# A decode attention block on one core: V as the stationary operand in every step, q broadcast and outputs written step by step

## The chip, the cores and the metric

The kernel runs on 1 core of one Trainium2 chip. The metric is the device time in microseconds of one execution; before the change the median of 3 runs is 1302.78 us (1302.27 to 1303.64).

A core has five engines with one instruction stream each: TensorE (PE; its weight loads are shown as PEld), VectorE (DVE), ScalarE (ACT), GpSimd (POOL) and SyncE (SP), which here issues nearly all transfers. They are ordered against each other by semaphores only. Transfers between HBM and the core's SBUF are carried out by sixteen DMA engines.

## The reference, cut to what matters

Eight sequences decode one token each. Attention has 32 heads, 4096 cached keys and a head size of 128; beside it stands a small MLP; all is bf16.

```python
def _A_ref(x, k_cache, v_cache, wq, wo):          # x (8,1,640), caches (8,32,4096,128)
    q = (x @ wq).reshape(B, Sq, Hq, Dh).transpose(0, 2, 1, 3)
    scores = jnp.einsum("bhqd,bhkd->bhqk", q, k) * (Dh ** -0.5)
    p = _softmax(scores, axis=-1)
    o = jnp.einsum("bhqk,bhkd->bhqd", p, v)
    return o.transpose(0, 2, 1, 3).reshape(B, Sq, Hq * Dh) @ wo

def _B_ref(x, w1, b1, w2, b2):
    y = _layernorm(x, axis=-1)
    h = _gelu(jnp.einsum("bsd,df->bsf", y, w1) + b1)
    return jnp.einsum("bsf,fd->bsd", h, w2) + b2

xn = _layernorm(x, axis=-1)
return x + _A_ref(xn, A_k_cache, A_v_cache, A_wq, A_wo) + _B_ref(xn, B_w1, B_b1, B_w2, B_b2)
```

The two caches are 2 x 268 MB; each element of them is used once.

## The kernel before

The work on the caches is cut into 64 steps (`NQ`): one step is one sequence `b` and a group of four heads (`HS`), 8 groups (`hq`) times 8 sequences. A step has 4 MiB of K and 4 MiB of V. Partition p holds head p // 32 and 128 consecutive keys of it, `j` = 0 to 127, so that `K_sb[p, slot, j, :]` is one key. K and V have two slots each (`i % 2`).

The keys of a step are shared by two ways to the scores. VectorE takes the first 88 (`dve_chunk`, four chunks of 22): it multiplies K by a q that is broadcast to the partitions of its head (`qbc_sb`), adds the two halves, and reduces. TensorE takes the last 40, in five tiles of 8 keys: `pe_T` transposes them to PSUM, `act_T` copies them to SBUF (`KT_sb`, `NS` = 4 buffers), `pe_QK` multiplies them by the four q columns, and `act_S` brings the scores home. `dve_max` finds the maximum per head over both shares, `act_exp` writes exp into `P_sb` and, by the accumulator, its row sums; `pe_RS` adds these over the partitions and `dve_rinv` inverts.

The product with V has P as the stationary operand: in `pe_PV` one matmul takes four keys of all partitions (`NA` = 32 matmuls of 512 columns in a step, issued in 8 groups), with a stationary operand of 16 columns, head by key. Of the 16 x 512 result only the blocks where the two key numbers agree are wanted: `act_E` evicts and scales it, and `pe_ex` picks the blocks with four small matmuls, into `OT_ps`. When the eight sequences of a head group are done, `cp_o` copies `OT_ps` out; `pe_ot` and `cp_ot` transpose it into rows of `O_sb`, and after seven groups `pe_ox` and `cp_ox` turn these into `oX_sb`, the stationary operand for the first 28 heads of `wo`. The last step (63) is written apart (`last_RS`, `last_PV`, `last_on` and others): there V is stationary, with 128 weight loads and a moving operand of 4 columns each, and the result is normalised on VectorE.

The q broadcast is made once for a head group: `qrep` on GpSimd repeats q along 32 columns for all 8 sequences (1024 columns), and two calls of `qbc` transpose it with matmuls, four sequences each, and copy it to `qbc_sb`.

The order on all engines is written by hand. `at(pos, fn)` gives each piece a position, step i lying at 100 i, and the pieces are recorded in the order of their positions. A recorder (`_Eng`) keeps each engine's list of calls and adds the waits, and `_replay` writes each list out. So an engine that waits at one piece holds up all that is later on its own list. On SP, K of step i is at 100 i - 90 and waits until step i - 2 is done with that slot (its transposes and VectorE's products), V of step i is at 100 i + 20 and waits for PV of step i - 2. The first part of `wo` (`load_woa`, 14 heads) is at 6222, behind V of step 62, and waits for `pe_ox`; V of step 63 is at 6320 in three pieces, and then come `wob` and the other four parts of `wo`. TensorE's list has in each step the transposes and QK tiles (from 100 i + 5), the q broadcast where one is due (+42), the row sums of the step before (+56), and its PV (+60). At the end stand `fin_b` and `fin_woa(0)`, the row sums and PV of step 63, `fin_wob` and the other `fin_woa`, and the store.

Of the kernel before, what the change touches and what calls it, by code (L numbers as in the profile page):

```python
# [92 lines left out]

def _replay(e, calls):
    for name, a, k, inc in calls:
        if name == "wait_ge":
            e.wait_ge(*a, **k)
            continue
        inst = getattr(e, name)(*a, **k)  # L99
        if inc is not None:  # L100
            inst.then_inc(*inc)


def bass_parallel_sum__gqa_block_cached__mixer_channel_mlp__decode_kernel(
# [28 lines left out]
    NPVG = 8  # L133
    NHA = H - HS
    NA = NKEY // 4
    assert NKEY == 128
    NS = 4
# [22 lines left out]
    with ExitStack() as es:  # L160
# [20 lines left out]
        P_sb = sb("P_sb", [P, 2, NA, HS, 4], BF)  # L181
        E_sb = sb("E_sb", [HS * 4, 2, 4 * DH], BF)
        qT_sb = sb("qT_sb", [P, H, B], BF)
        qrep_sb = sb("qrep_sb", [P, B, HS, HP], BF)
        qbc_sb = sb("qbc_sb", [P, 2, B, DH], BF)
        oTn_sb = sb("oTn_sb", [P, 2, HS, B], BF)
# [13 lines left out]
        mask_sb = sb("mask_sb", [P, HS * 4], F32)  # L200
# [6 lines left out]
        rs_sb = sb("rs_sb", [P, 2], F32)  # L207
        rs4_sb = sb("rs4_sb", [P, HS], F32)
        ri4_sb = sb("ri4_sb", [P, HS], F32)
        ones_f = sb("ones_f", [P, P], F32)  # L210
        rinv_sb = sb("rinv_sb", [HS * 4, 2], F32)
# [11 lines left out]
        OT_ps = CH_ps[:, 0:B * HS]  # L223
        RS_ps = CH_ps[0:HS * 4, 32:33]
# [71 lines left out]
        def consts_pool():  # L296
            tk["iota"] = pool.sig(pool.iota(iota_i[:, :], [[1, P]], base=0, channel_multiplier=-1))
            pool.memset(mask_sb[:, :], 0.0)
            pool.memset(zeros_sb[:, :], 0.0)
            pool.memset(ones_sb[:, :], 1.0)  # L300
            pool.memset(mx_sb[:, :], 0.0)
            pool.memset(rs4_sb[:, :], 0.0)
            pool.memset(ones_f[:, :], 1.0)
            t = pool.sig(pool.memset(nsc_sb[:, :], -SCALE))
            pool.wait(t)
            for h in range(HS):
                t = pool.sig(pool.memset(mask_sb[h * HP:(h + 1) * HP, h * 4:(h + 1) * 4], 1.0))
            tk["consts"] = t
            pool.wait(t)
            tk["pz"] = pool.sig(pool.memset(P_sb[:, :, :, :, :].rearrange("p n a h s -> p (n a h s)"), 0.0))  # L310
# [61 lines left out]
        def qrep(hq):  # L372
            pool.wait(tk[("q", hq * HS)], tk.get(("qb_pe", hq - 1)))
            tk[("qrep", hq)] = pool.sig(pool.tensor_copy(
                qrep_sb[:, :, :, :],
                qT_sb[:, hq * HS:(hq + 1) * HS, :].rearrange("p h b -> p b h")[:, :, :, None].to_broadcast(
                    [P, B, HS, HP])))

        def qbc(hq, half):
            k = trn[0] % 2  # L380
            trn[0] += 1
            pe.wait(tk[("qrep", hq)], tk["id"])
            TRB[k].use(pe)
            for bb in range(4):
                last = pe.matmul(TRF[:, k, bb * P:(bb + 1) * P],
                                 qrep_sb[:, half * 4 + bb, :, :].rearrange("p h r -> p (h r)"),
                                 ident_bf[:, :], start=True, stop=True)
            t = TRB[k].used(pe, pe.sig(last))
            tk[("qb_pe", hq)] = t
            act.wait(tk.get(("km", (hq - 1) * B - 1)))  # L390
            TRB[k].use(act)
            tk[("qb", hq, half)] = TRB[k].used(act, act.sig(act.activation(
                qbc_sb[:, hq % 2, half * 4:half * 4 + 4, :].rearrange("p b d -> p (b d)"),
                TRF[:, k, :], ACT.Copy)))
# [22 lines left out]
        def pe_QK(i, t):  # L417
            n = bank0[i] + t
            hq, b = divmod(i, B)
            s = i % 2  # L420
            pe.wait(tk[("ev", n)], tk[("q", hq * HS)])
            if t == 0:
                SB_[s].use(pe)
            for jj in range(TPB):
                c0 = (t * TPB + jj) * HS
                last = pe.matmul(S_ps[:, s, c0:c0 + HS], KT_sb[:, n % NS, jj, :],
                                 qT_sb[:, hq * HS:(hq + 1) * HS, b], start=True, stop=True)
            tk[("qk", n)] = SB_[s].used(pe, pe.sig(last))

# [10 lines left out]
        def dve_chunk(i, c):  # L440
            hq, b = divmod(i, B)
# [4 lines left out]
            dve.wait(piece_of("k", i, lo, hi), tk[("qb", hq, b // 4)], tk.get(("ya", n - 1)))  # L446
            tm = dve.sig(dve.tensor_tensor(
                Y_sb[:, 0:w, :], K_sb[:, s, lo:hi, :],
                qbc_sb[:, hq % 2, b, :][:, None, :].to_broadcast([P, w, DH]), ALU.mult))
# [23 lines left out]
        def act_exp(i):  # L473
            s = i % 2
            act.wait(tk[("nb", i)], tk.get(("pv", i - 2)), tk.get(("rs", i - 2)), tk["pz"])
            last_q = i == NQ - 1
            for h in range(HS):
                r = slice(h * HP, (h + 1) * HP)
                dst = (P_sb[r, s, :, :, :].rearrange("p a h s -> p (a h s)").rearrange(
                    "p (a s h) -> p a s h", s=4, h=HS)[:, :, :, h] if last_q else P_sb[r, s, :, h, :])  # L480
                last = act.activation(dst, Sd_sb[r, s, :].rearrange("p (a s) -> p a s", s=4),
                                      ACT.Exp, bias=NB_sb[r, s, 0:1], scale=SCALE,
                                      accum_out=rs4_sb[r, h:h + 1] if last_q else rs_sb[r, s:s + 1])
            tk[("exp", i)] = act.sig(last)

        def pe_RS(i):
            s = i % 2
            pe.wait(tk[("exp", i)])
            CHB.use(pe)
            tk[("rs", i)] = CHB.used(pe, pe.sig(pe.matmul(  # L490
                RS_ps, mask_sb[:, :], rs_sb[:, s:s + 1], start=True, stop=True)))

        def dve_rinv(i):
            CHB.use(dve)
            dve.wait(tk.get(("e", i - 2)))
            tk[("ri", i)] = CHB.used(dve, dve.sig(dve.reciprocal(rinv_sb[:, i % 2:i % 2 + 1], RS_ps)))


        def pe_PV(i, g):
            s = i % 2  # L500
            w = NA // NPVG
            if g == 0:
                pe.wait(tk[("exp", i)])
                PVB[s].use(pe)
            pe.wait(piece_of("v", i, g * w * 4, (g + 1) * w * 4))
            for a in range(g * w, (g + 1) * w):
                last = pe.matmul(PV_ps[0:HS * 4, s, :], P_sb[:, s, a, :, :].rearrange("p h s -> p (h s)"),
                                 V_sb[:, s, 4 * a:4 * a + 4, :].rearrange("p j d -> p (j d)"),
                                 start=(a == 0), stop=(a == NA - 1))
            if g == NPVG - 1:  # L510
                tk[("pv", i)] = PVB[s].used(pe, pe.sig(last))

        def act_E(i):
            s = i % 2
            act.wait(tk[("ri", i)], tk.get(("ex", i - 2)))
            PVB[s].use(act)
            tk[("e", i)] = PVB[s].used(act, act.sig(act.activation(
                E_sb[:, s, :], PV_ps[0:HS * 4, s, :], ACT.Copy, scale=rinv_sb[:, s:s + 1])))

        def pe_ex(i):  # L520
            s, b = i % 2, i % B
            pe.wait(tk[("e", i)], tk["id"])
            CHB.use(pe)
            for m in range(4):
                last = pe.matmul(OT_ps[:, b * HS:(b + 1) * HS], E_sb[:, s, m * P:(m + 1) * P],
                                 ident_bf[0:HS * 4, m:HS * 4:4], start=(m == 0), stop=(m == 3))
            tk[("ex", i)] = CHB.used(pe, pe.sig(last))

        def cp_o(hq):
            CHB.use(dve)  # L530
            dve.wait(tk.get(("ot", hq - 2)))
            tk[("o", hq)] = CHB.used(dve, dve.sig(dve.tensor_copy(
                oTn_sb[:, hq % 2, :, :].rearrange("p h b -> p b h"),
                OT_ps.rearrange("p (b h) -> p b h", h=HS))))

        def pe_ot(hq):
            pe.wait(tk[("o", hq)], tk["id"])
            ACCB.use(pe)
            for hh in range(HS):
                last = pe.transpose(OR_ps[0:B, hh * DH:(hh + 1) * DH], oTn_sb[:, hq % 2, hh, :], ident_bf[:, :])  # L540
            tk[("ot", hq)] = ACCB.used(pe, pe.sig(last))

        def cp_ot(hq):
            ACCB.use(act)
            act.wait(tk["mlp"])
            tk[("or", hq)] = ACCB.used(act, act.sig(act.activation(
                O_sb[:, hq * HS * DH:(hq + 1) * HS * DH], OR_ps[0:B, 0:HS * DH], ACT.Copy)))

        def pe_ox():
            pe.wait(*[tk[("or", hq)] for hq in range(NHQ - 1)])  # L550
# [9 lines left out]

        def zero_last():
            pool.wait(tk[("pv", NQ - 3)])
            tk["pz"] = pool.sig(pool.memset(
                P_sb[:, (NQ - 1) % 2, :, :, :].rearrange("p a h s -> p (a h s)"), 0.0))

        def last_RS():
            pe.wait(tk[("exp", NQ - 1)], tk["consts"])
            CHB.use(pe)
            CHB.used(pe, pe.sig(pe.matmul(CH_ps[:, 40:40 + HS], ones_f[:, :], rs4_sb[:, :],
                                          start=True, stop=True)))  # L570

        def last_rinv():
            CHB.use(dve)
            tk["ri4"] = CHB.used(dve, dve.sig(dve.reciprocal(ri4_sb[:, :], CH_ps[:, 40:40 + HS])))

        def last_PV(q):
            i, s = NQ - 1, (NQ - 1) % 2
            lo, hi = cuts("v", i)[q]
            if q == 0:
                PVB[s].use(pe)  # L580
            pe.wait(tk[("exp", i)], tk[("v", i, q)])
            ph = P_sb[:, s, :, :, :].rearrange("p a h s -> p (a h s)").rearrange("p (j h) -> p j h", h=HS)
            for j in range(lo, hi):
# [249 lines left out]
```

## Time and profile before

The profiled execution took 1300.0 us, its span (from the first to the last instruction) is 1298.2 us. Busy times are those of the span.

| | busy us | what it is mostly |
|---|---|---|
| profiled execution / its span / median of 3 runs | 1300.0 / 1298.2 / 1302.78 | |
| DVE, K times q | 410.2 in 255 instructions, 1609 ns | 22 keys each |
| DVE, reduction | 412.4 in 255, 1617 ns | |
| DVE, adding halves | 227.9 in 255, 894 ns | |
| PE, PV with P stationary | 576.6 in 2016, 512 columns | 9.4 to 9.9 us for the 32 of a step |
| PE, transposes of K | 191.5 in 2592 | |
| ACT, copies of transposed K | 317.8 in 324, 1022 ns | |
| ACT, exp | 101.6 in 256, 397 ns | |
| POOL, repeating q | 11.3 in 8, 1407 ns | |
| K load, 4 MiB | 64 loads | 24.7 us from issue to landing |
| V load, 4 MiB | 62 loads | 29.8 us from issue to landing |

A row of the costliest groups gives line, engine, operation, the tile written and those read, the shapes and the count, then the busy time and the mean duration of one in ns, and the idle time of the engine before them with what ended it. All the rows have line 99, since one helper writes every instruction; they are told apart by their tiles. Busy matmuls overlap, so the mean of one is longer than the time between two. The granted clock is the share of full speed that TensorE's clock had; its mean is 0.861.

### The profile page before, as it was taken

The numbers are of one execution on the slowest core, as the hardware profiler recorded it, in microseconds if no ns is written. First come the engines' busy times: TensorE is split into PE (matmuls) and PEld (weight loads), VectorE is DVE, ScalarE is ACT, GpSimd is POOL, SyncE is SP. The second block draws the span as 40 slices with busy tenths as digits, with TensorE's granted clock in tenths as the row PEclk, the third lists the DMA queues.
The fourth block names the chain that finished last, engine by engine and source line by source line (L and its number), as shares of the span: only waits on it lengthen the run. The fifth ranks groups of instructions, "written<-read, shape, count | busy, mean of one in ns | idle before, by whom it ended". The sixth has DMA issues, their size and how long they took to land.

```text
span 1298.2 us, 19364 instructions
## 1 busy us (share of the span) xinstructions
PE 919.8 (71%) x8239; PEld 477.8 (37%) x8239; DVE 1117.9 (86%) x1178; ACT 546.4 (42%) x1188; POOL 14.1 (1%) x26
## 2 busy tenths in 40 slices
PE   1778767767667767667767677677676677687688
PEld 1634333333333333333333333333333333343345
DVE  2998988988888988988979988888988989889883
ACT  1454353353453453453443443443543533534533
POOL 1000000000000000000000000000000000000000
PEclk9988788788888888798887888888887888888889
DMA  9999999999999999999999999999999999999997
GB/s 403 425 433 430 428 434 428 431 431 431 428 434 430 427 432 432 428 432 432 426 433 430 428 432 433 430 428 432 430 430 432 431 428 432 430 428 431 430 424 293
DMA packets 20762, 553.04 MB, mean 426 GB/s; under 512 B 2282, under 2 KB 3011, under 8 KB 3268
## 3 DMA queue, kind: packets, MB, share of 16 engines
q1 hardware_dynamic: 20642, 551.80, 99.1%
q8 instruction: 64, 1.05, 0.3%
q14 instruction: 22, 0.18, 0.0%
q10 hardware_dynamic: 34, 0.02, 0.0%
HBM read 551.80 MB, written 0.01 MB: 425 GB/s over the span
## 4 chain that ended last, share of the span: by engine, by line
DMA 67%; PE 23%; DVE 7%; ACT 2%; issue 1%; SPq 0%; DVEq 0%; ACTq 0%
DMA V_sb<-in_A_v_cache_dram 60%; PE PV_ps L99 22%; DMA K_sb<-in_A_k_cache_dram 8%; DVE Y_sb L99 4%; DVE Sd_sb L99 2%; ACT KT_sb L99 1%; PE S_ps L99 1%; ACT P_sb L99 0%; PE CH_ps L99 0%; PE TR_ps L99 0%; ACT E_sb L99 0%; DVE mx_sb L99 0%; DVE mb_sb L99 0%; DVE mxT_sb L99 0%; DVE NB_sb L99 0%
## 5 line engine op out<-in xcount | busy, mean ns | idle before, releaser
L99 PE MATMUL PV_ps<-V_sb,P_sb 128*16 128x512 bf16 x2016 | 576.6, 457 | 91.3 <-DMA V_sb<-in_A_v_cache_dram 91.3
L99 DVE TENSOR_TENSOR Y_sb<-K_sb,qbc_sb 128x2816 bf16<-128x2816 bf16 (+2 forms) x255 | 410.2, 1609 | 81.7 <-DMA K_sb<-in_A_k_cache_dram 81.6
L99 DVE TENSOR_REDUCE Sd_sb<-Y_sb 128x22 f32<-128x1408 bf16 (+2 forms) x255 | 412.4, 1617 | 8.7
L99 PEld LDWEIGHTS PV_ps<-V_sb,P_sb 128*16 128x16 bf16 x2016 | 204.3, 104 | 437.2 <-issue 183.7
L99 ACT ACTIVATE KT_sb<-TR_ps 128x1024 bf16<-128x1024 bf16 x324 | 317.8, 1022 | 78.0 <-PE TR_ps L99 76.8
L99 ACT ACTIVATE E_sb<-PV_ps,rinv_sb 16x512 bf16<-16x512 f32 x63 | 42.7, 677 | 621.6 <-PE PV_ps L99 611.4
L99 DVE TENSOR_TENSOR Y_sb<-Y_sb 128x1408 bf16<-128x1408 bf16 (+2 forms) x255 | 227.9, 894 | 8.7
L99 PE MATMUL TR_ps<-ident_bf,K_sb 128*128 128x128 bf16 x2592 | 191.5, 222 | 13.5 <-DMA K_sb<-in_A_k_cache_dram 10.7
L99 PE MATMUL S_ps<-qT_sb,KT_sb 128*128 128x4 bf16 x2592 | 118.4, 169 | 104.4 <-ACT KT_sb L99 93.7
L99 PEld LDWEIGHTS TR_ps<-ident_bf,K_sb 128*128 128x128 bf16 x2592 | 150.1, 99 | 16.0 <-DMA K_sb<-in_A_k_cache_dram 12.3
L99 PEld LDWEIGHTS S_ps<-qT_sb,KT_sb 128*128 128x128 bf16 x2592 | 89.1, 97 | 153.7 <-ACT KT_sb L99 151.7
L99 ACT ACTIVATE P_sb<-Sd_sb,NB_sb 32x128 bf16<-32x128 f32 x256 | 101.6, 397 | 7.7 <-DVE NB_sb L99 5.3
L99 PE MATMUL CH_ps<-rs_sb,mask_sb 128*16 128x1 f32 x126 | 13.0, 173 | 91.4 <-ACT P_sb L99 91.2
L99 PE MATMUL CH_ps<-ident_bf,E_sb 16*128 16x4 bf16 x252 | 15.6, 163 | 51.5 <-ACT E_sb L99 51.5
L99 ACT ACTIVATE Sd_sb<-S_ps 32x40 f32<-32x40 f32 (+2 forms) x256 | 49.7, 194 | 3.9 <-PE S_ps L99 0.5
L99 ACT ACTIVATION_READ_ACCUMULATOR P_sb<-Sd_sb,NB_sb 32x1 f32 x256 | 47.3, 185 | 0.0
L99 PEld LDWEIGHTS CH_ps<-rs_sb,mask_sb 128*16 128x16 f32 x126 | 7.5, 100 | 98.0 <-ACT P_sb L99 97.8
L99 PEld LDWEIGHTS CH_ps<-ident_bf,E_sb 16*128 16x128 bf16 x252 | 10.2, 91 | 82.4 <-ACT E_sb L99 82.4
L99 DVE TENSOR_REDUCE mx_sb<-Sd_sb 128x1 f32<-128x128 f32 x64 | 18.3, 285 | 5.9
L99 DVE CAST oTn_sb<-CH_ps 128x32 bf16<-128x32 f32 (+1 forms) x8 | 2.4, 295 | 23.4 <-PE CH_ps L99 23.4
L99 PE MATMUL CH_ps<-xT_sb,W_sb 128*128 128x8 bf16 (+1 forms) x230 | 11.1, 179 | 14.4 <-DMA W_sb<-in_A_wq_dram 10.8
L99 POOL COPY qrep_sb<-qT_sb 128x1024 bf16<-128x1024 bf16 x8 | 11.3, 1407 | 902.4 <-PE TR_ps L99 871.2
(71 smaller groups left out, 156.8 us busy)
## 6 DMA issues: line engine op xcount, KB each, us to landing
K_sb<-in_A_k_cache_dram SPq DMA_DIRECT2D x64, 4096.0 KB, 24.7
V_sb<-in_A_v_cache_dram SPq DMA_DIRECT2D x62, 4096.0 KB, 29.8
W_sb<-in_A_wq_dram SPq DMA_DIRECT2D x1, 5120.0 KB, 15.3
V_sb<-in_A_v_cache_dram SPq DMA_DIRECT2D x2, 2048.0 KB, 26.7
V_sb<-in_A_v_cache_dram SPq DMA_DIRECT2D x2, 1536.0 KB, 21.8
W_sb<-in_A_wo_dram SPq DMA_DIRECT2D x1, 2240.0 KB, 33.8
W_sb<-in_B_w_dram SPq DMA_DIRECT2D x1, 2160.0 KB, 15.7
W_sb<-in_B_w_dram SPq DMA_DIRECT2D x1, 2080.0 KB, 20.6
```

What stands on the lines that cost most here:

```text
L99: inst = getattr(e, name)(*a, **k)
```

## The change

- PV has V as the stationary operand in every step: for each of the 128 keys of a partition one weight load of V (128 x 128) and one matmul with the 4 columns of P. `P_sb` is laid out by key and then head, so exp writes every fourth element; row sums are kept per head (`rs4_sb`), and the result of `pe_RS` stands on all partitions. `act_E`, `pe_ex` and `cp_o` go; `act_O` evicts 128 x 4, and `o_norm` multiplies by the inverse sums on GpSimd (on VectorE in the last step) and writes into `oT_sb`, which has all heads.
- The q broadcast is made in every step for that step: `qrep` repeats 128 columns, `pe_qbc` transposes them with one matmul, `act_qbc` copies them. `pe_QK` takes its q columns from `qrep_sb`.
- `pe_ot` and `cp_ot` run in four groups of up to 8 heads at positions 6044 to 6185, and `pe_ox` at 6244. The first part of `wo` is at 6246. The last step no longer has functions of its own; exp of step 62 is at 6300.5, ahead of the transposes of step 63.
- `NS` is 5 instead of 4.
- A function is defined that replays a list as a loop (`_replay_loop`). It isn't called: TensorE's list is written out in full, as before. `marks` serves an assertion at build time only.

The diff, cut to its core:

```diff
@@ def qrep, qbc
-        def qrep(hq):
-            pool.wait(tk[("q", hq * HS)], tk.get(("qb_pe", hq - 1)))
...
-        def qbc(hq, half):
...
+        def qrep(i):
+            hq, b = divmod(i, B)
+            s = i % 2
+            pool.wait(tk[("q", hq * HS)], tk.get(("qb_pe", i - 2)), tk.get(("qkl", i - 2)))
+            tk[("qrep", i)] = pool.sig(pool.tensor_copy(
+                qrep_sb[:, s, :, :],
+                qT_sb[:, hq * HS:(hq + 1) * HS, b][:, :, None].to_broadcast([P, HS, HP])))
+
+        def pe_qbc(i):
             k = trn[0] % 2
             trn[0] += 1
+            pe.wait(tk[("qrep", i)], tk["id"])
             TRB[k].use(pe)
+            tk[("qb_pe", i)] = TRB[k].used(pe, pe.sig(pe.matmul(
+                TRF[:, k, 0:DH], qrep_sb[:, i % 2, :, :].rearrange("p h r -> p (h r)"),
+                ident_bf[:, :], start=True, stop=True)))
+            tk[("qbk", i)] = k
+
+        def act_qbc(i):
+            k = tk[("qbk", i)]
+            act.wait(tk.get(("km", i - 2)))
             TRB[k].use(act)
+            tk[("qb", i)] = TRB[k].used(act, act.sig(act.activation(
+                qbc_sb[:, i % 2, :], TRF[:, k, 0:DH], ACT.Copy)))
...
@@ def act_exp, pe_RS, dve_rinv, pe_PV
-                dst = (P_sb[r, s, :, :, :].rearrange("p a h s -> p (a h s)").rearrange(
-                    "p (a s h) -> p a s h", s=4, h=HS)[:, :, :, h] if last_q else P_sb[r, s, :, h, :])
-                last = act.activation(dst, Sd_sb[r, s, :].rearrange("p (a s) -> p a s", s=4),
+                last = act.activation(P_sb[r, s, :, h], Sd_sb[r, s, :],
                                       ACT.Exp, bias=NB_sb[r, s, 0:1], scale=SCALE,
-                                      accum_out=rs4_sb[r, h:h + 1] if last_q else rs_sb[r, s:s + 1])
+                                      accum_out=rs4_sb[r, s, h:h + 1])
...
-                RS_ps, mask_sb[:, :], rs_sb[:, s:s + 1], start=True, stop=True)))
+                RS_ps[:, s, :], ones_f[:, :], rs4_sb[:, s, :], start=True, stop=True)))
...
+        def pe_PV(i, q):
+            s = i % 2
+            lo, hi = cuts("v", i)[q]
+            if q == 0:
                 PVB[s].use(pe)
-            pe.wait(piece_of("v", i, g * w * 4, (g + 1) * w * 4))
-            for a in range(g * w, (g + 1) * w):
-                last = pe.matmul(PV_ps[0:HS * 4, s, :], P_sb[:, s, a, :, :].rearrange("p h s -> p (h s)"),
-                                 V_sb[:, s, 4 * a:4 * a + 4, :].rearrange("p j d -> p (j d)"),
-                                 start=(a == 0), stop=(a == NA - 1))
-            if g == NPVG - 1:
+            pe.wait(tk[("exp", i)], tk[("v", i, q)])
+            for j in range(lo, hi):
+                last = pe.matmul(PV_ps[:, s, 0:HS], V_sb[:, s, j, :], P_sb[:, s, j, :],
+                                 start=(j == 0), stop=(j == NKEY - 1))
+            if hi == NKEY:
                 tk[("pv", i)] = PVB[s].used(pe, pe.sig(last))
 
-        def act_E(i):
...
-        def pe_ex(i):
...
-        def cp_o(hq):
...
+        def act_O(i):
+            s = i % 2
+            act.wait(tk.get(("on", i - 2)))
             PVB[s].use(act)
+            tk[("oU", i)] = PVB[s].used(act, act.sig(act.activation(
+                oU_sb[:, s, :], PV_ps[:, s, 0:HS], ACT.Copy)))
+
+        def o_norm(i):
+            hq, b = divmod(i, B)
+            s = i % 2
+            dst = oT_sb[:, hq * HS:(hq + 1) * HS, b]
+            if i < NQ - 1:
+                pool.wait(tk[("oU", i)], tk[("ri", i)])
+                tk[("on", i)] = pool.sig(pool.tensor_tensor(dst, oU_sb[:, s, :], ri4_sb[:, s, :], ALU.mult))
+            else:
...
@@ the order
-                at(o + 20, load_v, i)
-            if b == 4 and hq + 1 < NHQ:
-                at(o + 50, qrep, hq + 1)
-                at(o + Q + 42, qbc, hq + 1, 0)
-                at(o + Q + 43, qbc, hq + 1, 1)
+                at(o + 20 if i != NQ - 2 else o + 20, load_v, i)
+            if i >= 1:
+                at(o - 60, qrep, i)
+                at(o - 58, pe_qbc, i)
+                at(o - 57.5, act_qbc, i)
...
-            at(o + Q + 39.5 if not last else o + 83, act_exp, i)
+            at(o + Q + 39.5 if i < NQ - 2 else o + Q + 0.5 if not last else o + 83, act_exp, i)
+            at(o + Q + 56, pe_RS, i)
+            at(o + Q + 57, dve_rinv, i)
+            for q in range(len(cuts("v", i))):
+                at(o + Q + 60 + q, pe_PV, i, q)
             if not last:
...
+                at(o + Q + 84, act_O, i)
+            at(o + Q + 88, o_norm, i)
...
-        at(o - 178, load_woa, 0)
+        for g in range(len(OTG)):
+            at(o - 356 + 47 * g, pe_ot, g)
+            at(o - 355.5 + 47 * g, cp_ot, g)
+        at(o - 156, pe_ox)
+        at(o - 155.5, cp_ox)
+        at(o - 154, load_woa, 0)
...
         @block.tensor
         def _(e):
+            assert len({y - x for x, y in zip(marks, marks[1:])}) == 1, marks
             _replay(e, pe.calls)
```

## The prediction

> **What bounds the kernel now.** First the rows of the page on transfers: the busy share in 40 slices, the rate under it, and the queues.
>
> ```profile
> span 1298.2 us, 19364 instructions
> PE 919.8 (71%) x8239; PEld 477.8 (37%) x8239; DVE 1117.9 (86%) x1178; ACT 546.4 (42%) x1188; POOL 14.1 (1%) x26
> ...
> DMA  9999999999999999999999999999999999999997
> ...
> q1 hardware_dynamic: 20642, 551.80, 99.1%
> q8 instruction: 64, 1.05, 0.3%
> ```
>
> The transfers are busy from end to end at about 430 GB/s, so no engine sets the pace; loading K and V does. The small row q8 decides this case. It carries TensorE's own program: PE and PEld have 2 x 8239 = 16,478 instructions, and 1.05 MB over 16,478 is 64 bytes each, so 64 packets of 16,384 bytes hold 256 instructions apiece (16,478 / 256 = 64.4). In the trace they come one every 20 us.
>
> Next, the table by stretches at the end (its columns: busy time and count of PE, PEld, DVE, ACT, POOL; granted clock; DMA share; GB/s).
>
> ```profile
> 1280.00:1282.00 2.00, 1.23 (x10) 0.46 (x9) 0.00 (x0) 1.28 (x5) 0.00 (x0) 1.00 0.99 402
> 1282.00:1284.00 2.00, 2.00 (x20) 1.50 (x20) 0.00 (x0) 0.00 (x0) 0.00 (x0) 1.00 0.63 263
> 1284.00:1286.00 2.00, 2.00 (x17) 1.27 (x16) 0.00 (x0) 0.00 (x0) 0.00 (x0) 1.00 0.63 259
> ...
> 1292.00:1294.00 2.00, 2.00 (x17) 1.30 (x15) 0.00 (x0) 0.00 (x0) 0.00 (x0) 1.00 0.32 118
> 1294.00:1296.00 2.00, 1.84 (x14) 0.96 (x11) 0.26 (x1) 0.13 (x1) 0.00 (x0) 1.00 0.00 0
> ```
>
> At 1282 us the share falls to 0.63, which is 10 of 16: six transfer engines are done and ten go on, the last until 1294.0. Each load leaves sixteen landing marks in the trace, one for each engine, and they tell why. At 35 us the sixteen marks of a load lie within 1.2 us of each other; at 595 us, after 29 refills, five engines are 6.1 to 6.5 us behind the first, three 4.8 to 5.0; at the end, after 64 refills, eight are 11.1 to 11.6 us behind. So the refills go round eight engines. The last mark of successive 4 MiB loads comes every 9.71 us, except around refills 9, 17, 25, 33, 41, 49 and 57, where it takes 11.10 to 11.16: a refill costs its engine 1.43 us, and the latest of the eight, hit every eighth time, sets when loads are complete.
>
> Last, the order of time on TensorE in the final 30 us:
>
> ```profile
> 1272.41 8.54 PE L99 MATMUL PV_ps<-V_sb,P_sb 128*16 128x512 bf16 x32
> ...
> 1287.15 3.37 PE L99 MATMUL PV_ps<-P_sb,V_sb 128*128 128x4 bf16 x128
> ...
> 1290.78 1.25 PE L99 MATMUL S_ps<-W_sb,oTn_sb 128*8 128x320 bf16 x8 [0.27 <-DVE oTn_sb L99]
> ...
> 1291.87 3.97 PE L99 MATMUL S_ps<-W_sb,oX_sb 128*8 128x320 bf16 x28
> ```
>
> The first row is P stationary (step 62), the second V stationary (step 63): the form that the change gives to every step is in the trace. PE ends at 1295.85, 1.9 us after the last landing.
>
> **The change, part by part.** *PV per step.* In steady state 32 matmuls take 9.4 to 9.9 us (rows at 605.07 and 624.50); 128 weight loads with 4 columns each take 3.24 us here. With a slower clock: 140 such pairs (8 columns) at 31 us, just after transposes at half pace (8 in 1.03 us, later 0.61), took 3.92 us, 28 ns a pair, so at most 3.6. TensorE gains about 6 us per step, plus 0.25 for the four extraction matmuls. What follows sooner is the next V load, which waits for PV; but the queue holds two and a half loads by then (24.7 us from K's issue to landing, at 9.71 us each), so the gain is 0. If that cover went, PE's 71% would leave the path free anyway.
>
> *TensorE's program.* 63 steps x 96 more pairs is 6048, less 252 extractions: 5796 pairs, 11,592 instructions, 45.3 more packets: 109 instead of 64. The diff defines a loop that would avoid this and does not call it. The latest engine, hit at 1, 9, ... 57 now, is hit also at 65, 73, 81, 89, 97 and 105: 6 x 1.43 = **+8.6 us** at the last landing. Bounds: five hits (7.2) or seven (10.0) if the count of waits among the instructions shifts it; and if a refill cost only its bytes, 16,384 at one engine's 4 MiB/16 per 9.71 us, it is 0.61 us, 3.6 in all. I take 1.43, since it is measured on this very queue.
>
> [...]
>
> *GpSimd.* One copy of 128 columns and one product of 4 columns per step, where there were eight copies of 1024 (1.407 us each). Bounds for each: 0.09 us (the smallest memset) to 1.41; 0.2 to 2.8 us per step on an engine that is 1% busy. I take the low end, nearer in size. They lie a step ahead: in the step shown, ScalarE copies a q broadcast at 603.02 and the next K's first product starts at 614.76, 11.7 us of cover. Behind a copy in GpSimd's queue stands only a product of a step that has long ended. Should they slow VectorE, the cover is its wait for K: 81.6 us over 54 waits, 1.5 each.
>
> *ScalarE.* Exp into every fourth element: 0.58 against 0.40 us, its accumulator read 0.25 against 0.185 (rows of steps 63 and 62): 4 x 0.245 = +1.0 per step. Evicting 128x4 instead of 16x512: 0.68 to about 0.19 (nearest row, 32x40). The q copy each step: +0.05 to +0.45. Net some +0.8 on 8.5 of 20 us; cover: PV waits 1.3 to 1.8 us for V after the row sums, and has 6 us to spare behind. *VectorE:* the reciprocal 0.146 to 0.182, seven casts go: nothing. *Head:* fewer broadcasts before K's landing at 25.8 us, which ends that wait anyway: 0.
>
> *Order at the end.* Transposes of the outputs move into steps 60 to 62, and the first wo load must wait for them, with V of step 63 and the other wo pieces behind it on SP's queue. They end about 8 us after K of step 62 lands (1242.5), so near 1250; V of step 62 keeps the late engines busy until 1271.7. 0. Exp of step 62 now precedes the transposes of step 63, so PV(62) runs early and in 3.2 us: PE then waits for landings alone. Counting from landings as now (V63 1286.9, wob 1288.5, wo pieces 1291.2, 1292.8, 1293.6, 1294.0) with 0.141 us a matmul (3.97 / 28): 8 matmuls after wob, 14 from 1291.2 to 1293.2, then 8, 4 and 2 end at 1295.2: **-0.65** against 1295.85.
>
> *Clock.* PE is then idle some 9 us before V63 lands. Against that, the profile grants 0.5 in single stretches now (0.70 as the mean of 1270 to 1275). The transposes at half pace are 1.95 times slower by their 7 intervals ((1.03 - 0.17) / (0.61 - 0.17)), so the last matmuls would take 0.275 us. Full clock: 0; all 36 at half: +3.7. I take a switch to full speed halfway, **+1.5**.
>
> [...]
>
> **Sum.** +8.6 - 0.65 + 1.5 = +9.5 us on a profiled time of 1300.0 (span 1298.2, 1.8 around it): 1309.5. The runs shown have a median of 1302.78, 2.8 above the profiled one; so 1312.3.
>
> **Rivals.** *Not slower:* V loads issued 6 us sooner let a load run faster than 9.71 us. For it: SP waits 293.6 us for PV. Against: the share stands at 0.99 to 1.03 in all stretches to 1282. 127 loads must each gain 0.075 us (0.8%) to cancel +9.5; 0.1 us would give 1299.6. Chance 0.10, two thirds of it within 0.2%. *Starved TensorE:* a V-stationary burst eats 256 instructions, a whole packet, in 3.24 us, and a packet takes 1.02 to 1.11 us once it is served; queued behind data it may come late. In mid-kernel there are 6 us for it; in the last two PV bursts each could lose 1 to 2.5: 1314 to 1317. For: no burst of that rate ran under full load yet. Chance 0.11. *VectorE as bound:* GpSimd's work at its upper price, 2.8 us per step, stretching VectorE beyond the 1.5 us that it waits: 64 x 1.3 = 83 us, 1396. Against: the operands are tiny. 0.03. *The packets spread over all sixteen engines, or count at 0.61:* +3.6 to +5, 1306 to 1308; 0.06.
>
> **How the numbers follow.** The forecast, 0.70, has its own range from five hits at full clock (7.2 - 0.65: 1309.3) to seven at half (10.0 - 0.65 + 3.7: 1315.8). Taking in the cheaper packets and the starved end gives 1306 to 1317; outside are the first rival and the third. 0.2% is 2.6 us, about what a measurement of this kernel can tell from no change: faster 0.03, same 0.08, slower 0.89.
>
> **What would show it.** q8 with about 109 packets and 1.8 MB; jumps of 1.43 us in the last marks about every eighth refill; the early engines some 19 us ahead and so idle late, a DMA share below 1 before the end; last landing near 1302.6; PV groups of 3.3 us with waits for V ahead of them. If q8 grows and the last landing stays at 1294, the price of a refill is wrong; if PV has idle time inside a burst, the second rival holds.

## The result, and the profile after

The changed kernel takes 1309.77 us (median of 5 runs, 1309.09 to 1310.56) against 1302.93 us (1302.27 to 1303.64) for the kernel before in the same comparison. The ratio is 1.0052, with a 95% interval of 1.0039 to 1.0065: about 6.8 us slower, and the interval is clear of the 0.2% that can be told from no change.

The page of the changed kernel, with the rows that answer to those shown of before (for q1, q8 and q14: packets, MB, share of sixteen engines):

```profile
span 1308.0 us, 31232 instructions
...
PE 677.6 (52%) x14035; PEld 605.4 (46%) x14035; DVE 1122.7 (86%) x1170; ACT 550.6 (42%) x1233; POOL 48.5 (4%) x139
...
PEclk9755555655555555555565555555555555555567
...
q1 hardware_dynamic: 20642, 551.80, 98.7%
q8 instruction: 110, 1.80, 0.6%
q14 instruction: 25, 0.20, 0.0%
```

TensorE has lost a quarter of its busy time, 920 to 678 us, and the kernel is slower all the same. The transfers of data (q1) are the same packets and bytes. What has grown is q8, TensorE's own program: 64 to 110 packets of 16 KB.

The end by stretches (time, busy time and count of PE, PEld, DVE, ACT, POOL; granted clock; DMA share; GB/s):

```profile
1288.00:1290.00 2.00, 2.00 (x13) 1.17 (x12) 0.00 (x0) 1.71 (x7) 0.16 (x1) 0.79 0.98 403
1290.00:1292.00 2.00, 2.00 (x17) 1.22 (x15) 0.00 (x0) 0.00 (x0) 0.06 (x1) 1.00 0.63 261
1292.00:1294.00 2.00, 1.34 (x50) 1.24 (x49) 0.18 (x1) 0.00 (x0) 0.00 (x0) 1.00 0.48 203
...
1302.00:1304.00 2.00, 2.00 (x15) 1.19 (x14) 0.00 (x0) 0.00 (x0) 0.00 (x0) 0.88 0.14 51
1304.00:1306.00 2.00, 1.62 (x12) 0.83 (x10) 0.48 (x1) 0.34 (x1) 0.00 (x0) 1.00 0.00 0
```

From 1292 us on only half of the sixteen engines (0.48) move data, for ten microseconds more; the last landing is at 1303.60. Before, it was at 1293.99. So the loss lies in front of the last landing, in the transfers, and not in TensorE's work behind it.

### The profile page after: what moved, and what is told of

It reads as the page before. It is cut to its first block, busy times and chain, and to the rows that moved or that the text cites. A ratio compares the mean times of both kernels' runs of the same rounds, so it can differ in the third digit from the quotient of the medians.

```text
span 1308.0 us, 31232 instructions
## 1 busy us (share of the span) xinstructions
PE 677.6 (52%) x14035; PEld 605.4 (46%) x14035; DVE 1122.7 (86%) x1170; ACT 550.6 (42%) x1233; POOL 48.5 (4%) x139
## 4 chain that ended last, share of the span: by engine, by line
DMA 64%; DVE 28%; issue 4%; PE 3%; ACT 1%; SPq 0%; DVEq 0%
DMA K_sb<-in_A_k_cache_dram 54%; DVE Y_sb L99 19%; DVE Sd_sb L99 8%; DMA V_sb<-in_A_v_cache_dram 5%; DMA W_sb<-in_A_wo_dram 3%; DMA W_sb<-in_B_w_dram 1%; PE PV_ps L99 1%; PE CH_ps L99 1%; PE TR_ps L99 1%; ACT KT_sb L99 1%; PE S_ps L99 0%; DVE ri_sb L99 0%; ACT P_sb L99 0%; PE ACC_ps L99 0%; SPq L99 0%
## 5 line engine op out<-in xcount | busy, mean ns | idle before, releaser
L99 PE MATMUL TR_ps<-ident_bf,K_sb 128*128 128x128 bf16 x2592 | 300.9, 297 | 386.8 <-DMA K_sb<-in_A_k_cache_dram 385.4
L99 PEld LDWEIGHTS TR_ps<-ident_bf,K_sb 128*128 128x128 bf16 x2592 | 240.9, 136 | 392.6 <-DMA K_sb<-in_A_k_cache_dram 391.0
L99 PE MATMUL PV_ps<-P_sb,V_sb 128*128 128x4 bf16 x8192 | 229.5, 166 | 19.2 <-DMA V_sb<-in_A_v_cache_dram 14.5
L99 PEld LDWEIGHTS PV_ps<-P_sb,V_sb 128*128 128x128 bf16 x8192 | 224.8, 104 | 22.3 <-DMA V_sb<-in_A_v_cache_dram 16.8
L99 PE MATMUL S_ps<-qrep_sb,KT_sb 128*128 128x4 bf16 x2592 | 122.9, 171 | 73.7 <-ACT KT_sb L99 69.5
L99 PEld LDWEIGHTS S_ps<-qrep_sb,KT_sb 128*128 128x128 bf16 x2592 | 101.2, 105 | 123.3 <-ACT KT_sb L99 120.3
L99 ACT ACTIVATE P_sb<-Sd_sb,NB_sb 32x128 bf16<-32x128 f32 x256 | 147.3, 575 | 12.1 <-DVE NB_sb L99 7.6
L99 PE MATMUL CH_ps<-rs_sb,ones_f 128*128 128x4 f32 x128 | 36.6, 356 | 124.1 <-ACT P_sb L99 122.2
L99 PEld LDWEIGHTS CH_ps<-rs_sb,ones_f 128*128 128x128 f32 x128 | 31.0, 301 | 130.3 <-ACT P_sb L99 128.0
L99 POOL TENSOR_TENSOR oT_sb<-oU_sb,ri_sb 128x4 bf16<-128x4 f32 x63 | 30.1, 478 | 1204.2 <-ACT oU_sb L99 1169.7
L99 POOL COPY qrep_sb<-qT_sb 128x128 bf16<-128x128 bf16 x64 | 20.9, 328 | 36.8 <-PE S_ps L99 22.3
```

## The experiments

The landing marks of all the kernels, read from the traces in one way: packets in q8 and q14, the last landing, how far the last of a load's sixteen marks is behind the first at the end, the span, and the median of the runs in us.

```
kernel                              q8   q14   last landing   lag   span     median
before, the first profile           64   22    1293.99       11.6   1298.2   1302.93
before, e0                          64   22    1294.18       11.9   1301.3   1303.10 (1 run)
changed                            110   25    1303.60       13.6   1308.0   1309.77
e4: products on VectorE            110   23    1303.12       13.3   1307.9   1309.65
e6: 14 passes of PE's loop          67   25    1295.38       13.5   1300.2   1302.32
e1: 28 passes of PE's loop          20   26    1291.41        9.5   1296.0   1297.79
e7: the same, idle pairs            27   25    1291.17        9.3   1296.6   1298.38
e5: loops on PE, DVE, ACT           20    9    1286.40        4.6   1291.3   1293.10
e9: e5 again                        20    8    1286.72        4.8   1291.2   1293.74
e8: e5, exp of step 62 late         20    8    1286.61        4.7   1290.8   1293.68
e3: before, waits on POOL           64   71    1315.03       10.7   1321.4   1324.64
e2: before, idle pairs on PE       110   22    1346.40        1.7   1370.3   1375.90
```

The theory was that refills of TensorE's program slow the late transfer engines, and so all loads. Rivals were the other parts of the change.

**e0: the kernel before, unchanged.**

> The kernel before, unchanged, for its trace beside the others of this call. In the first profile it took 1300.0 us, while its median in the comparison with the changed kernel is 1302.93. Theory (refills of TensorE's program set the last landing): 64 packets in q8, the last marks of 4 MiB loads 9.71 us apart with a jump of about 1.4 us at every eighth refill, last landing between 1294 and 1297. Rival (the pace of a load itself differs between executions): the plain interval differs from 9.71 by more than 0.02 us.

The last landing hardly moved (1294.18 against 1293.99), with jumps of 1.34 to 1.53 us at the eighth refills and 9.71 us otherwise. But the span is 3.1 us longer. The difference is behind the last landing; TensorE's order of time at the end of e0:

```profile
1291.24 2.29 PE L99 MATMUL S_ps<-W_sb,oTn_sb 128*8 128x320 bf16 x8 [0.27 <-DVE oTn_sb L99]
1293.33 5.62 PE L99 MATMUL S_ps<-W_sb,oX_sb 128*8 128x320 bf16 x28
```

The same 36 matmuls took 1.25 and 3.97 us in the first profile: there the granted clock was 1.00 from 1290 us on, here it is 0.50 in the stretch of 1290 to 1295 and 0.87 behind it. The five runs of before in the comparison, 1302.27 to 1303.64, go with e0 by their times, and the first profile (1300.0) had an end at a granted clock of 1.00. Between the two profiled spans (1301.3 and 1308.0) lie 6.7 us, close to the 6.8 between the medians: +9.4 us at the last landing (1294.18 to 1303.60) and -2.7 behind it (7.1 to 4.4 us from the last landing to the end of the span).

**e1: TensorE's steps as a loop.** All the work of the changed kernel, with fewer instructions to fetch:

```diff
-            _replay(e, pe.calls)
+            _replay_loop(e, pe.calls, marks[0], marks[-1], LOOPN)
```

> The changed kernel with TensorE's 28 middle pairs of steps replayed as a loop, by the function that the change defines; every engine does the same work. Theory: the loop is some 870 instructions; if TensorE's store holds them, q8 falls from 110 packets to 20 to 30, the latest engine is hit 3 or 4 times instead of 14, and the last landing comes 14 to 16 us sooner: 1293 to 1296 us, faster than the kernel before. If each pass fetches the loop again, q8 stays near 100 packets and the time at 1308 to 1312, more if TensorE stalls at the branch. Rival (V as stationary operand, GpSimd's work or the clock cost the time): 1309 to 1311 whatever q8 shows.

Its page:

```profile
q8 instruction: 20, 0.33, 0.1%
q14 instruction: 26, 0.20, 0.0%
```

1297.79 us, ratio 0.9962 to the kernel before (0.9950 to 0.9975): 12 us less than the changed kernel for the same work, so it is the fetching of the larger program (110 packets in q8 against 20) that costs. Eleven of the 20 refills come by 140 us and the other nine after 1204; none in between: while TensorE goes round the loop, q8 carries nothing. The gain at the last landing, 12.2 us, is less than the 14 to 16 expected. The marks tell why: a single engine is now 9.5 us behind the first, and the next 7.2. It falls back by 0.95 to 0.99 us at a time, shortly after every second of the 8 KB packets in q14. That these carry the programs of the other engines is what e5 and e3 test.

**e5: loops on VectorE and ScalarE too.**

```diff
+            at((LOOP0 + 2 * m) * Q, lambda: (dmarks.append(len(dve.calls)), amarks.append(len(act.calls))))
...
-            _replay(e, dve.calls)
+            _replay_loop(e, dve.calls, dmarks[0], dmarks[-1], LOOPN)
...
-            _replay(e, act.calls)
+            _replay_loop(e, act.calls, amarks[0], amarks[-1], LOOPN)
```

> The changed kernel with the 28 middle pairs of steps as a loop on TensorE, VectorE and ScalarE; every engine does the same work. With TensorE's loop alone the last landing was at 1291.4, and one transfer engine was 9.5 us behind the first, in jumps of 0.96 us that match the 8 KB refills in q14. Theory: those are VectorE's and ScalarE's programs; q14 falls from 26 packets to under 10, the latest engine is hit by TensorE's 20 packets alone, some 4 to 6 us behind the first, last landing 1286 to 1288, time 1291 to 1294. Rival (these engines lose at the branches or at waits against a register what the refills give back): 1297 to 1300 with q14 down.

```profile
span 1291.3 us, 33223 instructions
...
q8 instruction: 20, 0.33, 0.1%
q14 instruction: 9, 0.07, 0.0%
```

1293.10 us, ratio 0.9922 (0.9905 to 0.9939), as forecast. The lag is 4.6 us: 1.1 at the start, and three jumps of 0.89, 1.42 and 1.38 us in the last marks. This version beats both kernels: 10 us under the one before, 16.7 under the changed one. The loops lose nothing that shows.

**e6: half of the passes written out.** This asks what the change is worth with a program as large as before.

```diff
-    LOOP0, LOOPN = 4, 28
+    LOOP0, LOOPN = 4, 14
...
-            _replay(e, pe.calls)
+            _replay_loop(e, pe.calls, marks[0], marks[-1], LOOPN)
```

> The changed kernel with only 14 of the 28 pairs of steps as a loop on TensorE, the rest written out: q8 should come to some 63 to 66 packets, as before the change. So it shows what the change is worth without its larger program. Theory: last landing 1293 to 1296 as in the kernel before, and an end 2 to 3 us nearer to it (4.4 us of span behind the last landing against 7.1): 1299 to 1302. Rival (something else in the change costs time): 1305 or more.

```profile
q8 instruction: 67, 1.10, 0.3%
```

67 packets, last landing at 1295.38, and 1302.32 us, ratio 0.9993 (0.9983 to 1.0003), a shade above the range that was expected and far from the rival's 1305. The end lies 4.8 us behind the last landing, 2.3 nearer than in e0; the last landing is 1.2 us later than there, which three more packets, most of them in one half of the kernel, can explain; this was not tested by itself. So with a program of nearly the same size the change is worth nothing that can be measured, and its loss comes with the 46 packets more.

**e3: waits on GpSimd.** The kernel before with an instruction stream that does nothing (the 200 calls of a step stand in the trace as 100 instructions):

```diff
+        def pool_pad():
+            for _ in range(200):
+                pool.wait_ge(*tk["consts"])
+
+        for i in range(1, NQ):
+            at(i * Q + 30, pool_pad)
```

> The kernel before with some 6300 instructions more on GpSimd that only wait for a semaphore long since reached, 100 per step: about 49 more packets of 8 KB in q14, none in q8. It tells whose engine a refill loads. If the packets of one instruction stream all go to one transfer engine that is early now, that engine falls behind the late eight: 49 x 0.6 to 0.8 us less its lead of up to 11.6 us, 1315 to 1335 us. If they go round eight or sixteen engines: 1303 to 1308. If only TensorE's stream counts: 1302 to 1304.

```profile
q8 instruction: 64, 1.05, 0.3%
q14 instruction: 71, 0.58, 0.1%
```

1324.64 us, ratio 1.0171 (1.0151 to 1.0191), from 0.4 MB of waits. The last marks now jump by 0.65 us some forty times, and at the end one mark is 10.7 us behind the first, the next only 3.5: 49 packets go to one transfer engine, 49 x 0.65 = 32 us, less a lead of some 11 that it had, and 21.7 were measured. So here a stream refilled on one engine is dearer per byte (20.9 us at the last landing for 0.4 MB) than TensorE's, which goes round eight (9.4 us for the 0.75 MB of the changed kernel's 46 packets).

**e2: idle pairs on TensorE.** The kernel before with the number of pairs that the change adds, behind the extraction matmuls:

```diff
+            for _ in range(92):
+                last = pe.matmul(CH_ps[:, 400:404], ident_bf[:, :], ident_bf[:, 0:4], start=True, stop=True)
             tk[("ex", i)] = CHB.used(pe, pe.sig(last))
```

> The kernel before with 92 idle pairs of weight load and 4-column matmul in each of 63 steps, behind the extraction matmuls and into unused PSUM: 63 x 92 = 5796 pairs, the number that the change adds, and nothing else of the change. Theory: 109 or 110 packets in q8, last landing 8.6 to 9.7 us later, time 1309 to 1313. Rival (the other parts of the change cost the time): 1302 to 1304, as 2.3 us more of TensorE per step fit into its idle time.

A miss by both theories: 1375.90 us, ratio 1.0574 (1.0550 to 1.0597). The chain of waits of this run, and TensorE's order of time in one step:

```profile
PE 69%; ACT 25%; DMA 3%; issue 3%; DVE 0%; ACTq 0%; SPq 0%
```

```profile
616.97 8.70 PE L99 MATMUL PV_ps<-V_sb,P_sb 128*16 128x512 bf16 x32
626.50 0.25 PE L99 MATMUL CH_ps<-ident_bf,E_sb 16*128 16x4 bf16 x4 [0.83 <-ACT E_sb L99]
626.68 2.45 PE L99 MATMUL CH_ps<-ident_bf 128*128 128x4 bf16 x92
629.00 1.05 PE L99 MATMUL TR_ps<-ident_bf,K_sb 128*128 128x128 bf16 x16
```

No row waits for a transfer: TensorE and ScalarE go round without one, and a step takes 20.43 us (606.07 to 626.50) in place of 19.4. The kernel before had a ring of transposes, evictions, exp, row sums and PV that was only the 1.3 to 1.8 us shorter than a step that PV waited for V; 2.45 us do not fit. The pairs also slow what follows: eight transposes take 1.01 us here and 0.61 in the kernel before, and the mean granted clock is 0.781 instead of 0.857 (e0). The run doesn't tell the price of refills, since transfers no longer set the pace (a lag of 1.7 us).

**e7: the same idle pairs in the changed kernel,** behind PV, with TensorE's loop:

```diff
+                if i < NQ - 1:
+                    CHB.use(pe)
+                    for _ in range(92):
+                        last = pe.matmul(CH_ps[:, 400:404], ident_bf[:, :], ident_bf[:, 0:4],
+                                         start=True, stop=True)
+                    CHB.used(pe, pe.sig(last))
```

> The changed kernel with TensorE's loop and in each of 63 steps the same 92 idle pairs that, put into the kernel before, made it 1375.9 us, here behind PV. Its TensorE has 6 us less to do per step. Theory (TensorE stood close to the pace in the kernel before, and the change gives it room): 1297 to 1300, as with the loop alone (1297.79). Rival (idle pairs themselves cost the time, by refills or by the clock): 1340 or more.

```profile
603.60 3.57 PE L99 MATMUL PV_ps<-P_sb,V_sb 128*128 128x4 bf16 x128 [0.28 <-DMA V_sb<-in_A_v_cache_dram]
607.03 2.59 PE L99 MATMUL CH_ps<-ident_bf 128*128 128x4 bf16 x92
613.31 1.89 PE L99 MATMUL TR_ps<-ident_bf,K_sb 128*128 128x128 bf16 x16 [3.69 <-DMA K_sb<-in_A_k_cache_dram]
```

1298.38 us, ratio 0.9964 (0.9950 to 0.9978), as with the loop alone: behind the idle pairs TensorE still waits 3.69 us for K. So neither the pairs nor the clock (0.576 here, 0.583 in e1) cost time where TensorE has room. What V stationary gives is this room, which the loads don't ask for.

**e4: the products on VectorE.** GpSimd's product and ScalarE's eviction are taken out of the changed kernel; VectorE multiplies from PSUM:

```diff
-            if i < NQ - 1:
+            if False:
                 pool.wait(tk[("oU", i)], tk[("ri", i)])
...
-            if not last:
-                at(o + Q + 84, act_O, i)
```

> The changed kernel with every step's product with the inverse sums on VectorE, straight from PSUM (as its last step has it), instead of an eviction on ScalarE and a product on GpSimd. Theory (the time went to refills of TensorE's program; GpSimd's work is covered): no change, 1309 to 1311, q8 at 110, last landing at 1303 to 1304. Rival (GpSimd's work beside VectorE costs the time): 1302 to 1305.

1309.65 us, ratio 1.0050 (1.0033 to 1.0067): no change.

**e8 and e9: the order at the end.** The kernel with three loops, with exp of step 62 where the kernel before has it, beside the three loops again:

```diff
-            at(o + Q + 39.5 if i < NQ - 2 else o + Q + 0.5 if not last else o + 83, act_exp, i)
+            at(o + Q + 39.5 if not last else o + 83, act_exp, i)
```

> The kernel with three loops (1293.1 us), with exp of step 62 back behind the evictions of step 63, where the kernel before has it. It undoes the one reordering at the end that the forecast priced. Theory (TensorE waits for landings alone at the end): exp, row sums and VectorE's last chunk of step 63 come 1 to 3 us later and are still ahead of the last V piece; the time changes by less than 0.7 us against the three loops in this call. Rival (the reordering is what brought the end nearer to the last landing): 1.5 to 3 us slower, and the last matmuls no longer wait for landings.

> The changed kernel with three loops once more, beside the one with exp of step 62 in its old place: 1292 to 1294 us, 0.990 to 0.994 of the kernel before, q8 at 20 packets, last landing 1286 to 1287.

1293.68 and 1293.74 us, ratios 0.9923 (0.9909 to 0.9936) and 0.9929 (0.9916 to 0.9943): no difference. The end on TensorE with exp late:

```profile
1277.64 3.37 PE L99 MATMUL PV_ps<-P_sb,V_sb 128*128 128x4 bf16 x128
1281.33 1.96 PE L99 MATMUL S_ps<-W_sb,oT_sb 128*8 128x320 bf16 x8 [0.32 <-DVE oT_sb L99]
1283.93 4.53 PE L99 MATMUL S_ps<-W_sb,oX_sb 128*8 128x320 bf16 x28 [0.63 <-DMA W_sb<-in_A_wo_dram]
```

and with exp early (e5):

```profile
1279.34 1.00 PE L99 MATMUL PV_ps<-P_sb,V_sb 128*128 128x4 bf16 x32 [1.10 <-DMA V_sb<-in_A_v_cache_dram]
1281.09 2.29 PE L99 MATMUL S_ps<-W_sb,oT_sb 128*8 128x320 bf16 x8 [0.75 <-DMA W_sb<-in_A_wo_dram]
1283.69 5.26 PE L99 MATMUL S_ps<-W_sb,oX_sb 128*8 128x320 bf16 x28 [0.31 <-DMA W_sb<-in_A_wo_dram]
```

PV of step 63 no longer waits for V in the first, but both wait for the pieces of wo before the last group. So the nearer end of the changed kernel doesn't come from this order. What is left is PV of step 62, at 3.4 to 3.6 us in place of 8.5 to 8.8; no run tests it by itself.

## Why the prediction was right, and where not

- *The larger program, the main step: right in mechanism, under by 0.8 us.* 110 packets came where 109 were worked out. The last landing went from 1294.18 (e0) to 1303.60, +9.4 instead of +8.6. A round of the eight engines costs some 1.55 us (about 21 us in excess of 9.71 per load, over 110 / 8 rounds), slightly above the 1.43 taken from single jumps; 6 x 1.55 is 9.3. That it is the number of packets and not the other work is shown by e1 and e6, in which every engine does the work of the changed kernel with 20 and 67 packets.
- *TensorE itself loses little to its program:* in the changed kernel, with 110 packets in q8, the idle time before PV for which the profile shows no other reason ("issue") is 4.6 us in all. The time of the kernel is lost in the transfers: 0.20 us per packet at the last landing (9.4 us over 46).
- *The step that failed: the end, "-0.65" and "+1.5", with the "2.8 above the profiled one".* Against the first profile the sum is nearly met: +9.5 forecast, +9.8 measured (9.6 at the last landing, 0.2 behind it; the changed kernel's end does have a granted clock of 0.50, from 1296 to 1302 us). But the sum then adds the 2.8 us by which the median lies above that profile, as if they stayed. They don't: in e0 the kernel before runs the first of its last 36 matmuls at a granted clock of 0.50 (8 in 2.29 us, against 1.25), behind a PV of 8.75 us, and needs 7.7 us for the 36 where the first profile shows 5.1, so that its span is 3.1 us longer. The slow end was thus counted twice, as part of the median and as the +1.5 that the change would bring. The switch halfway behind the +1.5 was the author's choice between two bounds, and the profile before does not show one there; in the changed kernel the granted clock is 0.50 when the 36 begin and 1.00 from 1302.5 us on, and they take 2.29 and 4.74 us where the first profile has 1.25 and 3.97. Against e0 the end gained 2.7 us where +0.85 was forecast, a miss of some 3.6; the last landing missed by 0.8 the other way, which leaves about the 2.5 us between 1312.3 and 1309.77.
- *PV per step:* 3.58 us in mid-kernel, at a granted clock of 0.50, inside the 3.24 to 3.6 that were forecast, and worth nothing, as forecast. (That a slower clock set the pace of the pairs behind the 3.6 was the author's estimate, from transposes that took 1.03 us in place of 0.61; the table of stretches has 1.00 there, from 30 to 35 us.) But in "if that cover went, PE's 71% would leave the path free anyway" the reason doesn't hold: e2 shows that idle pairs of 2.45 us per step cost 73 us. A share of 71% hid a ring that was almost as long as a step.
- *GpSimd:* 0.33 us for the copy and 0.48 for the product, 0.8 per step; e4 shows that the product is covered. *ScalarE:* +0.8 us per step was forecast; its busy time rose by only 4.2 us in all, 546.4 to 550.6. The forecast added up rows that overlap: in the profile before, the exps of step 62 start 0.50 us apart and those of step 63 0.59, so the new layout costs 0.36 us a step and not 1.0.
- *Early engines "some 19 us ahead":* only 13.6. From 710 us on the lag stays between 12.0 and 13.9, and the first marks of the last load come 7.6 us later than before (1290.04, 1282.43). The early engines run out of issued loads, as loads are issued by what the late ones land: at 811.3 and 830.7 us the next load is issued only 1.3 and 2.0 us before their mark of the load ahead of it, and their next mark comes after 10.4 and 10.8 us instead of 9.71. That this costs nothing, as forecast, is not tested by itself.
- *The rivals.* Loads that go faster because V is issued sooner: the plain interval stayed at 9.71 us. (The share of 0.99 to 1.03 that spoke against it holds from 35 us on; in the first 35 us the stretches lie between 0.73 and 1.08.) VectorE as the bound: its busy time is 1122.7 against 1117.9 us. TensorE starved of instructions: six waits before PV have no other reason in the profile:

```profile
PE PV_ps L99 <- issue: 4.6, 6, 2.3
```

  4.6 us in total, up to 2.3 at once, and each time PV goes on 1.2 to 1.6 us after a packet of q8 has ended. None of the six is in the last two PV bursts, where the rival priced them; the last is at 1146 us.

Open is why a refill of TensorE's program takes its engine 1.4 to 1.55 us when its 16 KB, at the pace of data, would take 0.61; and which transfer engine each stream uses, since the marks don't name them. Packets of TensorE's program alone were never added to the kernel before: e2, which was to do it, came up against TensorE's own pace.

## What to carry to other kernels

In a kernel that is bound by its loads, as this one is, the size of the instruction streams can be part of the load: here 46 more packets of 16 KB put the last landing 9.4 us later. Look at the rows of the instruction queues, and at how far the sixteen landing marks of a load drift apart. Repeating steps whose instructions are the same can then be worth more as a loop than an engine's time saved: here TensorE's busy time fell by 242 us, and the change cost 7 us written out and gained 10 as three loops. The gain is the loops': with a program of nearly the old size (e6) the change was worth nothing, and no run shows the kernel before as loops. The end of an execution was a matter of the clock as well (the same 36 matmuls took 5.1 us at a granted clock of 1.00, and 7.7 us in e0, where it was 0.50 at first), so a sum is better made against a profile that takes as long as the median run than against a fast one with the difference added.

## What the runs showed of the hardware

- By the landing marks, each refill held back one of the sixteen marks of a load: TensorE's 16 KB packets went round eight, 1.4 to 1.55 us each (the kernel before and the changed one); GpSimd's 8 KB packets all went to one, 0.65 us each (e3); and every second 8 KB packet of q14 cost one mark 0.95 to 0.99 us (e1).
- A loop of some 870 instructions on TensorE ran through its 28 passes without a packet in q8 (e1, none between 140 and 1204 us).
- A larger busy share did not come with a higher granted clock. In e2 the small idle pairs bring TensorE from 71% to 80% busy, with no longer waits than before in mid-kernel (up to 1.5 us), and its mean granted clock goes from 0.857 to 0.781. With V stationary the clock is 0.568 at 52% busy; there small matmuls and waits of some 6 us for K in each step come together, and the runs don't part them.
- Pairs of 128 columns of weights and 4 columns of data lost little at the lower clock: 128 of them took 3.37 us at a granted 1.00 (the kernel before, step 63) and 3.58 at 0.50 (the changed kernel, at 629 us). Matmuls of 320 columns took nearly twice as long: 8 in 1.25 us at 1.00 (the kernel before), in 2.29 at 0.50 (e0 and the changed kernel).
